# Short filler matmuls left out of the first round of a routing search

## The chip, the cores and the metric

The kernel runs on one core of one Trainium2 chip. The metric is the time of one execution on the device in microseconds (us), and the kernel before has a median of 460.77 us over three runs (459.94, 460.78 and 460.77). One of these executions was also profiled. Where the text names an engine, PE is the matmul engine (TensorE), PEld its weight loads, DVE is VectorE, ACT is ScalarE, POOL is GpSimd and SP is SyncE, which issues most of the DMAs.

## The reference

Two blocks follow each other. The first is a gated linear attention: for each of 4 batches and 8 heads a 48x48 state is decayed and updated over 768 tokens.

```python
f = 1.0 / (1.0 + np.exp(-f_logit))
for t in range(S):
    state = f[:, :, t, :, None] * state + np.einsum('bhd,bhe->bhde', k[:, :, t], v[:, :, t])
    y[:, :, t] = np.einsum('bhd,bhde->bhe', q[:, :, t], state)
```

Its output, as x with 3072 rows of 384, goes into a layer of 8 experts. Each token gets one expert, and each expert takes exactly 384 tokens: all 3072 x 8 logits are walked from the largest to the smallest, and a pair is taken if its token is still free and its expert still has room.

```python
logits = x @ w_gate
for idx in np.argsort(-logits.flatten()):
    tok, e = int(idx) // E, int(idx) % E
    if assigned[tok] >= 0 or counts[e] >= cap:
        continue
    assigned[tok] = e
    counts[e] += 1
for e in range(E):
    out[assigned == e] = np.maximum(x[assigned == e] @ w1[e], 0.0) @ w2[e]
```

## The kernel before

**Attention.** The sequence is cut into 24 chunks of 128 tokens, and a software pipeline of six stages works on them (`attention`). The order of the instructions on PE, DVE, ACT and POOL is written out by hand, so each engine executes in program order and waits only for the semaphores of its operands. A finished chunk's x is copied to DRAM, transposed, and multiplied with the gate weights into `logits` (L387). While the pipeline runs dry, the kernel already prepares the first round of the routing for the 20 tiles of tokens that are done: each token's best logit, its choice of expert and its place on a scale of thresholds (`begin`, `part`, `at_steps`). The last chunk's four tiles follow when its logits arrive, and the 20 others are counted by PE in the meantime (L703); `need` is what is left of the wanted count behind these.

**Routing.** The walk over sorted logits is replaced by seven rounds (`rnd` 0 to 6). In each round every free token proposes to its best open expert, and a search finds the level of logit above which one expert becomes full. The search goes through five digits of the level (`search`). For one digit, `digit_alone` (L770) makes on DVE the comparison `above` with 16 thresholds, lets PE count the choices above each threshold (L780: 24 matmuls of 8 columns, four in the first digit of round 0, because `counted` holds the rest), compares the counts with the wanted number on DVE (`fills`, `filled`), and turns the result into a digit with one matmul of one column (L793). DVE's next comparison reads this digit. `assign` (L857) then marks the tokens above the level, sums them with a matmul (L869) and updates `taken` and `places`. `expert_list` makes the list of the full expert's tokens, starts the load of its weights (L959, SP) and gathers its rows of x (`xe`, L1030, POOL).

**Experts.** `ffn` makes a list of PE pieces for the expert: three transposes of gathered rows (`turn`, L1060), 24 matmuls up (`up`, L1071) and 24 down (`down`, L1083), all of 384 columns in fp32. They go into the queue `pe_work`, and `some(pe_work, n)` takes n pieces of it between the steps of the next rounds' searches. In round 0 there is no expert yet, so `pe_work` is empty until the first list is made.

**Filler.** `idle_turns(n, bank, size)` (L124) issues n matmuls of bf16 ones, `size` columns wide, into a PSUM bank that nobody reads; L127 is their line. Width 384 is used in the attention's start, behind the pieces of the first list (one after each, and 13 behind them) and in two digits of round 1. Width 128 is used in round 0 only: in `digit_alone` 12 ahead of the first digit's counts and 6 ahead of each other digit's counts (L776), 4 ahead of each digit's last matmul (L791), and in `assign` 12 ahead of the sum (L866). That is 12 + 4 x 6 + 5 x 4 + 12 = 68. The condition in `digit_alone` is `not turns[1]`; the first two digits of round 1 have `turns` of (0, 1) and keep their two wide filler matmuls. An exact version of the routing, which uses the same functions, lies behind a condition and does not run on these inputs.

Of the kernel before, what the change touches and what calls it, by code (L numbers as in the profile page):

```python
# [26 lines left out]
def kernel(  # L27
# [32 lines left out]
    nc = tc.nc  # L60
# [12 lines left out]
    CAP = N // E  # L73
# [17 lines left out]
    def const(shape, dtype, name):  # L91
        return consts.tile(shape, dtype, name=name, tag=name)
# [8 lines left out]
    ones = const([128, 128], BF16, "ones")  # L101
    idle = const([128, CAP], BF16, "idle")
# [18 lines left out]
    k_bufs = [kept([128, H, DP], FP32, f"kg{i}") for i in range(NB)]  # L121
    a_bufs = [kept([128, 2, HP, 128], FP32, f"am{i}") for i in range(NB)]

    def idle_turns(n, nothing, size=CAP):  # L124

        for _ in range(n):
            nc.tensor.matmul(out=nothing[:, 0:size], lhsT=ones[:], rhs=idle[:, 0:size], start=True,  # L127
                             stop=True)

    def constants():  # L130
# [67 lines left out]
    def sums(G):  # L198
        g = g_bufs[G["i"] % NB]
        if G["i"] == STAGES - 1:  # L200

            idle_turns(3, ps("nothing", "sum"))
        G["L"] = L = ps("L")
        Lv = L[:, 0:D].rearrange("t (h d) -> t h d", d=DH)
        if "terms" in G:
            for n, term in enumerate(G["terms"]):
                nc.tensor.matmul(out=L[:, 0:D], lhsT=wcum_r[:],
                                 rhs=term[:].rearrange("t h d -> t (h d)"),
                                 start=(n == 0), stop=(n == 1))
        else:  # L210
            nc.tensor.matmul(out=Lv, lhsT=wcum[:], rhs=g[:, :, 0:DH], start=True, stop=True)
# [44 lines left out]
    def columns(G, nm, t):  # L256
        if G["i"] in (1, 2):
            idle_turns(4, ps("nothing", "sum"))
        G[nm + "s"] = T = ps("T")
        for hp in range(HP):  # L260
            nc.tensor.transpose(
                out=T[:, 128 * hp:128 * hp + 128],
                in_=G[t][:, 2 * hp:2 * hp + 2, :].rearrange("t h d -> t (h d)"),
                identity=ident[:])
        G[nm] = work.tile([128, HP, 128], FP32, name=nm, tag=nm, bufs=3)
# [183 lines left out]
    in_order.__enter__()  # L449
    constants()  # L450
    idle_turns(19, ps("nothing", "sum"))
    clamp(chunks[0])
    attention(0, 2)
# [82 lines left out]
    def col(t, *shape):  # L536

        return t.rearrange("p (c o) -> p c o", o=1).to_broadcast((128, NT) + shape)
# [5 lines left out]
    def by_e(t):  # L544

        return t[:].rearrange("p c e -> p e c")

    def rt(shape, name, dtype=FP32, bufs=2):
        return route.tile([128] + shape, dtype, name=name, tag=name, bufs=bufs)
# [4 lines left out]
    def tt(out_, a, b, op):  # L554
        nc.vector.tensor_tensor(out=out_, in0=a, in1=b, op=op)
# [5 lines left out]
    def stt(out_, a, s, b, op0, op1):  # L561
        nc.vector.scalar_tensor_tensor(out=out_, in0=a, scalar=s, in1=b, op0=op0, op1=op1)  # L562

    def reduce(out_, in_, op):
        nc.vector.tensor_reduce(out=out_, in_=in_, axis=AX_X, op=op)
# [143 lines left out]
    def assign_and_run(begun=None, also=None, again=None, exact=None):  # L709
# [5 lines left out]
        def bank(name, tag):  # L715
            return psum.tile([128, 512], FP32, name=name, tag=tag, bufs=BUFS[tag])
# [5 lines left out]
        pe_work, dve_work = deque(), deque()  # L722

        def some(queue, n):
            for _ in range(min(n, len(queue))):
                queue.popleft()()
# [28 lines left out]
        def take(over, pick, level=0.0, op=ALU.is_ge):  # L755
            new = rt([NT], "new")
            stt(new[:], over, level, pick[:], op, ALU.mult)
            tt(taken[:], taken[:], new[:], ALU.add)
# [11 lines left out]
        def digit_alone(above, parts, choice, unit, counted=None, turns=(0, 0)):  # L770

            some(pe_work, turns[0])
            r = bank("cnt", "r")
            cols = [c for c in range(NT) if not counted or c % NCH == NCH - 1]
            if not turns[1]:
                idle_turns(12 if counted else 6, bank("nothing", "O"), 128)  # L776
            for c in cols:
                if c % 8 == 0 and not counted:
                    parts(c, c + 8)
                nc.tensor.matmul(out=r[0:NTH, 0:E], lhsT=above[:, c, :], rhs=choice[:, c, :],  # L780
                                 start=(c == cols[0]), stop=(c == cols[-1]))
            fills = rt([E], "fills")
            tt(fills[0:NTH, :], r[0:NTH, 0:E], counted[1][0:NTH, :] if counted else
               wanted[0:NTH, :], ALU.is_ge)
            filled = rt([1], "filled", BF16)
            reduce(filled[0:NTH, :], fills[0:NTH, :], ALU.max)
            if turns[1]:
                some(pe_work, turns[1])
                idle_turns(2, bank("nothing", "O"))
            else:  # L790
                idle_turns(4, bank("nothing", "O"), 128)  # L791
            digit = r[:, 128:129]
            nc.tensor.matmul(out=digit, lhsT=unit[0:NTH, :], rhs=filled[0:NTH, :], start=True,  # L793
                             stop=True)
            return digit, ALU.add
# [34 lines left out]
        def search(choice, over, digits, slots, first=0, counted=None, alone=()):  # L830


            def less(over, digit, op):
                if digit is None:
                    return over
                new = rt([NT], "over")
                ts(new[:], over[:], digit, op)
                return new

            digit = op = None  # L840
            for n, (steps, unit, size) in enumerate(digits):
                above = counted[0] if counted else rt([NT, NTH], "above", BF16)
                parts = partial(reached, above, over, digit, op, steps)
                if slots and n >= len(alone):
                    parts(0, NT)
                    new = less(over, digit, op)
                    digit, op = digit_beside(above, choice, size, (slots[0] + first, slots[1]))
                    over = new
                else:
                    new, op_new = digit_alone(above, parts, choice, unit, counted,  # L850
                                              *alone[n:n + 1])
                    over = less(over, digit, op)
                    digit, op = new, op_new
                first, counted = 0, None
            return less(over, digit, op) if exact else (over, digit)

        def assign(choice, over, pick, slots):  # L857

            over, level = over
            sure = rt([NT, E], "sure", BF16)  # L860
            stt(sure[:], col(over[:], E), level, choice[:], ALU.is_ge, ALU.mult)
            count = rt([E], "count", BF16)
            with nc.allow_low_precision("counts of at most 24"):
                reduce(count[:], by_e(sure), ALU.add)
            if not pe_work:
                idle_turns(12, bank("nothing", "O"), 128)  # L866
            some(pe_work, slots[0])
            r = bank("sums", "r")
            nc.tensor.matmul(out=r[:, 0:E], lhsT=ones[:], rhs=count[:], start=True, stop=True)  # L869
            some(pe_work, slots[1])  # L870
            take(over[:], pick, level)
            tt(places[:], places[:], r[:, 0:E], ALU.subtract)
# [175 lines left out]
        tiles, turns = iter(range(NT)), iter(range(E))  # L1048
# [52 lines left out]
        with tc.manual_schedule(engines=engines):  # L1101
# [5 lines left out]
            for rnd in range(E - 1):  # L1107
# [15 lines left out]
                else:  # L1123
                    counted = None
                    if rnd == 0:
                        choice, over, pick, _, *counted = begun
                    else:
                        best, pick, masked = picks()
                        choice, over = choices(best, pick, masked)
                        for piece in settle:  # L1130
                            piece()

                    over = search(choice, over, digits, slots, more, counted,
                                  ((0, 1), (1, 1)) if rnd == 1 else ())
                (assign_exact if exact else assign)(choice, over, pick, (3, 5 if rnd == 1 else 7))
                *pieces, used = expert_list(rnd == 0)
                dve_work.extend(pieces)
# [151 lines left out]
    with tc.If(again[0] > 0):  # L1289
# [9 lines left out]
        with tc.For_i(0, B, 1) as b:  # L1299
            x = pool.tile([128, NCH, D], FP32, name="xb", tag="xb", bufs=1)  # L1300
            with tc.For_i(0, HP, 1) as hp:
                scan_pair(pool, x, b, hp)
            nc.sync.dma_start(
                out=xd[0:N, :].rearrange("(b c t) d -> b t c d", b=B, c=NCH)[
                    bass.ds(b, 1)].rearrange("b t c d -> (b t) c d"),
# [13 lines left out]
        out=outs[NT - 1][:, :],  # L1319
# [31 lines left out]
```

## Time and profile before

| what | value |
|---|---|
| median of three runs | 460.77 us (459.94, 460.78, 460.77) |
| time of the profiled execution | 459.94 us |
| its span, first to last instruction | 458.1 us (1.84 us lie around it) |
| PE busy | 443.3 us, 97% of the span |
| DVE busy | 265.7 us, 58% |
| ACT, POOL busy | 139.3 us and 136.1 us, 30% each |
| mean granted TensorE clock | 0.975 of full speed |

The execution has three stretches. Attention lasts to about 151 us. The first round's search and its list of tokens follow. From about 178 us PE works on the experts' matmuls, with the later rounds' searches between them, until 451 us. In the profile a row of the timeline names the start and the duration of a merged group of instructions, its engine, its line, what it writes and reads, how many there are, and in brackets how long the engine had been idle and what ended that. A row of the windows names a stretch, its length, the busy time of each engine with the number of instructions, and the granted clock of PE (1.00 is full speed).

### The profile page before, as it was taken

The numbers are of one execution on the slowest core, as the hardware profiler recorded it, in microseconds if no ns is written. First come the engines' busy times: TensorE is split into PE (matmuls) and PEld (weight loads), VectorE is DVE, ScalarE is ACT, GpSimd is POOL, SyncE is SP. The second block draws the span as 40 slices with busy tenths as digits, with TensorE's granted clock in tenths as the row PEclk, the third lists the DMA queues.
The fourth block names the chain that finished last, engine by engine and source line by source line (L and its number), as shares of the span: only waits on it lengthen the run. The fifth ranks groups of instructions, "written<-read, shape, count | busy, mean of one in ns | idle before, by whom it ended". The sixth has DMA issues, their size and how long they took to land. (4 is left out here: it accounts for less than half of the span.)

```text
span 458.1 us, 12040 instructions
## 1 busy us (share of the span) xinstructions
PE 443.3 (97%) x4961; PEld 299.3 (65%) x4961; DVE 265.7 (58%) x879; ACT 139.3 (30%) x323; POOL 136.1 (30%) x189
## 2 busy tenths in 40 slices
PE   8999999999999989999999999999999999999994
PEld 4788888888887745565565565565565565556552
DVE  5789877788986586657547547647637636000000
ACT  4666666666551001202202212212212212212210
POOL 1566565565550021032032033023023025101001
PEclk9999999999999659999999999999999999999999
DMA  9999989899311036082072072082082087400001
GB/s 160 189 208 208 195 179 207 182 204 193 76 37 54 20 112 217 3 309 69 12 289 80 9 287 84 2 291 86 1 293 74 13 292 240 177 17 34 1 19 39
DMA packets 118400, 59.13 MB, mean 129 GB/s; under 512 B 101664, under 2 KB 112960, under 8 KB 118336
## 3 DMA queue, kind: packets, MB, share of 16 engines
q1 hardware_dynamic: 111760, 44.06, 38.5%
q0 software_dynamic: 3072, 9.44, 6.2%
q10 hardware_dynamic: 3504, 4.77, 3.0%
q8 instruction: 41, 0.67, 0.6%
q14 instruction: 23, 0.19, 0.1%
HBM read 48.77 MB, written 9.49 MB: 127 GB/s over the span
## 5 line engine op out<-in xcount | busy, mean ns | idle before, releaser
L1071 PE MATMUL H<-xeT,w 128*128 128x384 f32 x384 | 132.6, 496 | 0.1
L1071 PEld LDWEIGHTS H<-xeT,w 128*128 128x128 f32 x384 | 69.1, 190 | 45.7 <-issue 4.0
L1083 PE MATMUL O<-w,hT 128*128 128x384 f32 x192 | 67.0, 491 | 0.0
L1083 PE MATMUL last_O<-w,hT 128*128 128x384 f32 x192 | 66.7, 491 | 0.0
L1075 ACT ACTIVATE hT<-H 128x384 f32<-128x384 f32 x64 | 31.4, 491 | 101.3 <-PE H L1071 85.3
L1083 PEld LDWEIGHTS last_O<-w,hT 128*128 128x128 f32 x192 | 35.1, 190 | 23.1 <-issue 2.2
L1083 PEld LDWEIGHTS O<-w,hT 128*128 128x128 f32 x192 | 34.9, 190 | 21.5 <-issue 1.3
L1088 POOL DMA_INDIRECT out_dram<-o,token x21 | 21.3, 1013 | 82.2 <-ACT o L1087 81.3
L324 DVE COPY_PREDICATED am<-mask,A 128x512 f32<-128x512 int32 x48 | 32.3, 725 | 16.2 <-PE A L319 16.2
L988 POOL TENSOR_TENSOR block<-past 128x72 f32<-128x72 f32 x8 | 2.4, 302 | 114.3 <-DVE at L562 101.0
L190 POOL TENSOR_TENSOR low<-g,upper 128x384 fp32r<-128x384 f32 x22 | 22.3, 1014 | 42.5 <-DVE upper L188 38.9
L127 PE MATMUL nothing<-idle,ones 128*128 128x384 bf16 (+1 forms) x142 | 28.4, 354 | 2.4 <-DVE ones L132 1.5
L1063 ACT COPY xeT<-Xe 128x384 f32<-128x384 f32 x24 | 11.4, 480 | 59.7 <-PE Xe L1060 59.4
L334 PE MATMUL Y<-v,am 128*64 128x48 f32 x768 | 27.6, 223 | 1.0 <-DVE am L324 0.9
L334 PEld LDWEIGHTS Y<-v,am 128*64 128x64 f32 x768 | 24.8, 138 | 2.0 <-DVE am L324 1.6
L319 PE MATMUL A<-qT,kT 48*64 48x128 f32 x768 | 25.8, 272 | 0.0
L1030 POOL DMA_INDIRECT xe<-xd,token x21 | 21.5, 1023 | 12.4 <-DVE full L559 5.8
L243 POOL TENSOR_TENSOR kg<-k,ek 128x384 f32<-128x384 f32 x23 | 23.3, 1014 | 2.2 <-ACT ek L221 2.1
L319 PEld LDWEIGHTS A<-qT,kT 48*64 48x64 f32 x768 | 21.0, 133 | 0.4 <-issue 0.3
L127 PEld LDWEIGHTS <-ones 128*128 128x128 bf16 x142 | 14.3, 124 | 9.8 <-issue 6.3
L220 ACT ACTIVATE eq<-dl 128x384 f32<-128x384 f32 x24 | 12.5, 523 | 26.2 <-DVE dl L218 26.1
L1087 ACT COPY o<-O 128x384 f32<-128x384 f32 x12 | 5.7, 479 | 40.7 <-PE O L1083 30.0
(228 smaller groups left out, 668.2 us busy)
## 6 DMA issues: line engine op xcount, KB each, us to landing
w<-in_moe_w_dram SPq DMA_DIRECT2D x16, 1536.0 KB, 6.5
f<-in_f_logit_dram SPq DMA_DIRECT2D x24, 192.0 KB, 5.1
q<-in_q_dram SPq DMA_DIRECT2D x24, 192.0 KB, 5.0
k<-in_k_dram SPq DMA_DIRECT2D x24, 192.0 KB, 4.4
v<-in_v_dram SPq DMA_DIRECT2D x24, 192.0 KB, 5.0
xd<-x ACTq DMA_DIRECT2D x24, 192.0 KB, 2.4
xe<-xd,token POOLq DMA_INDIRECT x21
out_dram<-o,token POOLq DMA_INDIRECT x21
```

The source lines that it names most:

```text
L127: nc.tensor.matmul(out=nothing[:, 0:size], lhsT=ones[:], rhs=idle[:, 0:size], start=True, stop=True)
L190: nc.gpsimd.tensor_tensor(out=low[:], in0=g[:, :, 0:DH], in1=upper[:].bitcast(FP32), op=ALU.subtract)
L220: nc.scalar.activation(out=G["eq"][:], in_=dl[:], func=AF.Exp, bias=0.0, scale=-1.0)
L243: engine.tensor_tensor(out=G["kg"][:, :, 0:DH], in0=G["k"][:], in1=G["ek"][:], op=ALU.mult)
L319: nc.tensor.matmul(out=A[par][HC * j:HC * j + HC, 128 * hp:128 * hp + 128], lhsT=G["kT"][rows, hp, HC * j:HC * j + HC], rhs=G["qT"][rows, ...
L324: nc.vector.copy_predicated(am[:, par], mask[:].unsqueeze(1).to_broadcast((128, HP, 128)), A[par][:].rearrange("s (a t) -> s a t", t=128))
L334: nc.tensor.matmul(out=Y[par][HC * j:HC * j + HC, DH * hp:DH * hp + DH], lhsT=G["am"][:, par, hp, HC * j:HC * j + HC], rhs=G["v"][:, 2 * h ...
L1030: nc.gpsimd.indirect_dma_start(out=xe[:], out_offset=None, in_=xd[:, :], in_offset=bass.IndirectOffsetOnAxis(ap=token[:, i:i + 1], axis=0))
L1071: nc.tensor.matmul(out=L["H"][:, 0:CAP], lhsT=L["w1"][:, d, 128 * ft:128 * ft + 128], rhs=xT[:, d, :], start=(d == 0), stop=(d == DC - 1))
L1075: nc.scalar.activation(out=hT[:, ft, :], in_=L["H"][:, 0:CAP], func=AF.Relu)
L1083: nc.tensor.matmul(out=L["O"][:, 0:D], lhsT=hT[:, ft, 128 * i:128 * i + 128], rhs=L["w2"][:, ft, :], start=(ft == 0), stop=(ft == FC - 1))
L1088: nc.gpsimd.indirect_dma_start(out=outs[next(tiles)][:, :], out_offset=bass.IndirectOffsetOnAxis(ap=L["token"][:, i:i + 1], axis=0), in_=o ...
```

## The change

All 68 filler matmuls of 128 columns are left out, and `idle_turns` loses its argument for the width. The filler of 384 columns stays everywhere. Nothing else is edited; no operation is moved or added.

```diff
-    def idle_turns(n, nothing, size=CAP):
+    def idle_turns(n, nothing):
 
         for _ in range(n):
-            nc.tensor.matmul(out=nothing[:, 0:size], lhsT=ones[:], rhs=idle[:, 0:size], start=True,
+            nc.tensor.matmul(out=nothing[:, 0:CAP], lhsT=ones[:], rhs=idle[:], start=True,
                              stop=True)
...
             cols = [c for c in range(NT) if not counted or c % NCH == NCH - 1]
-            if not turns[1]:
-                idle_turns(12 if counted else 6, bank("nothing", "O"), 128)
             for c in cols:
...
             if turns[1]:
                 some(pe_work, turns[1])
                 idle_turns(2, bank("nothing", "O"))
-            else:
-                idle_turns(4, bank("nothing", "O"), 128)
             digit = r[:, 128:129]
...
                 reduce(count[:], by_e(sure), ALU.add)
-            if not pe_work:
-                idle_turns(12, bank("nothing", "O"), 128)
             some(pe_work, slots[0])
```

## The prediction

> **What bounds the kernel now.** I read the page first, for the clock and the filler's group.
>
> ```profile
> PEclk9999999999999659999999999999999999999999
> ...
> L127 PE MATMUL nothing<-idle,ones 128*128 128x384 bf16 (+1 forms) x142 | 28.4, 354 | 2.4 <-DVE ones L132 1.5
> ```
>
> PE has its full clock everywhere but in two slices, 149 to 172 us: just where the first round's search runs. The 142 filler matmuls include the 68 narrow ones. Next, one row of the windows, from the first expert matmul almost to the end:
>
> ```profile
> 178.46:448.00 269.54, 268.89 (x1117) 156.16 (x1118) 125.45 (x491) 52.42 (x108) 53.50 (x58) 1.00 0.33 116
> ```
>
> PE is busy 268.89 of 269.54 us. So from 178.46 us on PE alone sets the time, and whatever makes this stretch start earlier ends the kernel earlier by as much. Its start hangs on a chain: search, list, gather, first transposes. The transposes wait at 175.10 us for the gathered rows; PE sat idle 0.74 us before them, released by the DMA of xe. The gather and the weights' load are issued from results of the list, the list from the search. So the search of round 0 is on the path, and the timeline must say what ends last in it.
>
> ```profile
> 152.16 0.14 DVE L555 TENSOR_TENSOR need<-wanted,counted 16x8 f32<-16x8 f32 x1
> ...
> 152.36 1.44 PE L127 MATMUL nothing<-idle,ones 128*128 128x128 bf16 x12 [0.66 <-DVE need L555]
> 152.44 0.19 DVE L565 TENSOR_REDUCE pick<-masked 128x4 f32<-128x32 bf16 x1
> ...
> 153.73 0.25 PE L780 MATMUL cnt<-choice,above 128*16 128x8 bf16 x4
> ...
> 154.08 0.15 DVE L555 TENSOR_TENSOR fills<-cnt,need 16x8 f32<-16x8 f32 x1 [1.45 <-PE cnt L780]
> ```
>
> Here the filler itself ends last. The comparison `above` was done at 152.25 us, but the four counts stand behind 12 filler matmuls that start at 152.36 us and take 1.44 us. DVE, finished with `pick` at 152.63, waits 1.45 us. One later digit:
>
> ```profile
> 156.66 0.81 PE L127 MATMUL nothing<-idle,ones 128*128 128x128 bf16 x6
> 156.76 0.89 DVE L562 SCALAR_TENSOR_TENSOR above<-over,cnt,steps 128x128 bf16<-128x128 f32 x3 [0.16 <-PE cnt L793]
> 157.41 0.75 PE L780 MATMUL cnt<-choice,above 128*16 128x8 bf16 x24
> 158.09 0.61 PE L127 MATMUL nothing<-idle,ones 128*128 128x128 bf16 x4
> 158.19 0.15 DVE L555 TENSOR_TENSOR fills<-cnt,wanted 16x8 f32<-16x8 f32 x1 [0.55 <-PE cnt L780]
> 158.38 0.15 DVE L565 TENSOR_REDUCE filled<-fills 16x1 bf16<-16x8 f32 x1
> 158.63 0.18 PE L793 MATMUL cnt<-filled,unit 16*128 16x1 bf16 x1
> 158.85 0.89 DVE L562 SCALAR_TENSOR_TENSOR above<-over,cnt,steps 128x128 bf16<-128x128 f32 x3 [0.16 <-PE cnt L793]
> ```
>
> A digit's period is 158.85 - 156.76 = 2.09 us: `above` 0.89, from its end (157.65) to `fills` 0.54, to the end of `filled` (158.53) 0.34, and 0.32 to the next comparison. Round 1 has a digit with no filler ahead of its counts:
>
> ```profile
> 176.12 0.89 DVE L562 SCALAR_TENSOR_TENSOR above<-over,cnt,steps 128x128 bf16<-128x128 f32 x3 [1.38 <-PE cnt L793]
> 176.53 0.88 PE L780 MATMUL cnt<-choice,above 128*16 128x8 bf16 x24
> ...
> 177.45 0.15 DVE L555 TENSOR_TENSOR fills<-cnt,wanted 16x8 f32<-16x8 f32 x1 [0.44 <-PE cnt L780]
> ```
>
> There the counts start 0.11 us after the first third of `above`, and `fills` comes 0.44 us behind its end. Last, the windows, cut where the clock changes:
>
> ```profile
> 148.71:152.12 3.41, 2.62 (x79) 2.24 (x79) 1.88 (x9) 0.58 (x2) 0.00 (x0) 1.00 0.18 62
> 152.12:155.53 3.41, 3.17 (x36) 2.53 (x35) 1.64 (x9) 0.00 (x0) 0.16 (x3) 0.50 0.00 0
> 155.53:158.95 3.42, 3.42 (x65) 2.75 (x62) 1.94 (x11) 0.00 (x0) 0.00 (x0) 0.50 0.02 5
> ...
> 165.77:169.19 3.42, 2.66 (x30) 1.06 (x29) 3.02 (x8) 0.00 (x0) 1.29 (x2) 0.50 0.29 59
> 169.19:172.60 3.41, 3.35 (x16) 1.43 (x14) 2.97 (x13) 0.00 (x0) 2.13 (x2) 0.50 0.99 405
> ```
>
> The clock falls to 0.50 at 152.12 us, before the first narrow filler matmul runs, and stays there for 20.48 us, though PE counts as busy throughout 155.53 to 158.95. It rises at 172.60, after a stretch filled with matmuls of 384 columns. So the narrow filler runs at half clock, 1.44 us for twelve, and does not bring the clock back.
>
> **The change, part by part.**
>
> *12 matmuls ahead of the first counts.* Without them the counts can start when `above` (152.25) and `need` (152.30) are done, so about 152.36, where the filler starts now. They take 0.25, and `fills` follows 0.10 later (153.98 to 154.08 now): 152.71. DVE is free at 152.63 and not later. Gain 154.08 - 152.71 = 1.37 us. Bounds: 1.2, if the counts wait another 0.2 for their weights, as some rows show ("0.20 <-issue"); 1.4, if `pick` alone decides.
>
> *6 ahead of the counts and 4 ahead of the digit, in four digits.* The six end their weight loads just ahead of the counts' start, so counts for the first third of `above`, ready at 157.06, start at 157.41. By the round 1 rows `fills` would come 0.44 behind `above` in place of 0.54; these ran at full clock, but 24 counts' weight loads take 0.65 to 0.66 us at both clocks, so I take 0.46. Ahead of the digit's matmul the four cost little: from the end of `filled` to the next comparison 0.32 us, in the first digit 0.25 (154.42 to 154.67). I take 0.25. The period becomes 0.89 + 0.46 + 0.34 + 0.25 = 1.94, a gain of 0.15, and four periods (154.67 to 163.02) give 0.60 us. Bounds: 0.2, if only half of the counts' term comes and nothing of the other; 0.7, with 0.44. The four in the first digit end as `filled` ends: no gain.
>
> *12 ahead of the sum.* They run from 162.93 while DVE makes `sure` and `count`. `count` ends at 163.97, the sum starts at 164.17 and `places` at 164.45. Without filler the sum would start some 0.06 behind (191.33 to 191.39 in the next round) and end by 164.21, but `taken` keeps DVE until 164.34. Gain 0.05, bounds 0 and 0.1.
>
> *What follows.* Between `places` and the gather everything hangs on DVE, POOL and SP; the wide filler between it is unedited, and DVE does not wait for it. The weights' load (SP, 166.99) and the gathers (POOL, 170.01) come earlier by the same amount and collide with nothing else: DMA moves 0 to 5 GB/s from 152 to 159 us. Nothing is queued behind a new wait, since none is added. The list and the first transposes keep their length, so the next wait is again the gather's.
>
> Sum: 1.37 + 0.60 + 0.05 = 2.02 us, bounds 1.4 and 2.2, if the clock rises as now. Against the profiled execution, 459.94 us (458.1 of span and 1.84 around it), that is 457.9. This execution was the fastest of the three and lies 0.83 under the median; the other two may carry something that its trace doesn't show. Against the median it is 458.75, which I take.
>
> *The clock.* The three changes in the trace fit a grid: the wide filler's weight loads go from one in 0.32 us to six in 0.94 us at about 5.3 us, and 152.12 and 172.60 lie 43 and 49 steps of 3.413 us behind it. 169.19 to 172.60 is filled with wide matmuls from end to end. In 152.12 to 155.53 the narrow filler streams about 22 times 0.107 us (the twelve's spacing), 2.35 us or 69%, and the clock stayed at half. The share that suffices lies between.
>
> The Trainium skill's page "TensorE: Matmul & The Clock Gate" (Part 1 and "HAM oscillation") speaks against the edit: PE should have no idle gaps above about 3.4 us, or it falls to half clock, and single matmuls of N columns then take (219 + N)/1.2 instead of (398 + N)/2.4 ns. The rows show the fall in spite of the filler, so here the rule has nothing left to protect in the search. If the filler did hold the clock, the rule would charge 20 ns for each of two matmuls in five digits, an estimate of 0.2 us, and the sum would be 1.8. The page also says that the window is free-running, not tied to the program's start; no run here shows that yet.
>
> **The rivals.**
>
> *The rise is missed, and the kernel is slower.* The 14 wide filler matmuls behind the list need 14 x 0.32 = 4.48 us at half clock and start now at 169.18. They would start at 167.16 and end at 171.64. With the grid at the same place, 165.77 to 169.19 would hold 2.03 us of them and two single ones (0.64), 78%, and 169.19 to 172.60 would hold 2.45 us, 72%. Both lie between 69% (not enough) and 100% (enough); where they aren't, PE enters round 1 at half clock. Nine transposes (three in 0.55 us, about 0.13 more each) and four wide filler matmuls (0.16 more each) cost up to 1.8, say 1.5 us. The first expert matmuls, at about 178.0 then, run at half speed to the end of the first filled window, 182.84: (182.84 - 178.0)/2 = 2.4. Together 3.9 against 2.0: slower by 1.9, 461.8 from the profiled execution and 462.7 from the median. For it: the arithmetic of the shares. Against it: it needs the grid at the same place in every run, and three runs of before lie within 0.84 us, so none shows such a loss against another. It decides where the share that suffices is above 78%.
>
> *Half of that.* The clock is caught one window earlier, at 179.43, by the transposes and the first expert matmuls (176.01 to 179.43 has PE busy 3.28 us): 1.5 + 0.7 = 2.2 us, no change, 460.8 to 461.
>
> *Hidden anyway.* The expert stretch could hang on something that doesn't move, as a DMA with its own clock. Both transfers are issued from the list, so I see none: 460.8.
>
> **How the numbers follow.** About 0.2%, 0.92 us, is what can be told from no change. The forecast needs only the serial order on PE and gets 0.62, with its own range of 457.7 (459.94 less 2.2) to 459.4 (median less 1.4). The middle cases together get 0.13, the missed rise 0.25. The range goes down to 457.7 and up into the missed rise, to 462.2, between its two prices.
>
> **What would show it.** Right: `fills` of the first digit within 0.1 us of `pick`'s end, where it is 1.45 us behind now; digit periods of 1.9 to 1.95 us; first transposes about 23.0 us behind the first `need`'s row (152.16) become 20.9; PE from the first expert matmul on as dense and as long as before. Wrong in the steps: digit periods still at 2.09 (then the counts wait for DVE alone), or a first count that waits for something other than `need`. Wrong in the outcome: PEclk at 0.50 beyond the gathered rows' arrival, seen as transposes of far more than 0.55 us for three and expert matmuls at double their 0.34 us spacing.

## The result, and the profile after

The changed kernel has a median of 458.85 us over four runs (457.93 to 459.30), beside 460.77 us before (459.94 to 460.79). The ratio is 0.996 with a 95% interval of 0.9941 to 0.9979. The whole interval lies under 1, so the kernel is faster, by some 0.4%. A later comparison, with 12 runs of after and 23 of before, gave 459.70 and 463.36 us, a ratio of 0.9929 (0.9899 to 0.9959). So the sign is sure, and the size depends on something that the first profile alone does not show. The profile tells it by stages, cut at `need`, at `places`, at the first expert matmul and at the span's end:

| profiled execution | attention, to `need` | search, `need` to `places` | list, to the first expert matmul | experts, to the end | span |
|---|---|---|---|---|---|
| before | 152.16 | 12.29 | 14.01 | 279.6 | 458.1 |
| after | 154.47 | 10.06 | 13.34 | 279.6 | 457.5 |

The search is 2.23 us shorter, the list 0.67. The attention, which the change does not touch, happens to be 2.31 us longer in this execution of after, so the two profiled spans lie only 0.6 us apart. From here on stages are compared, not spans.

The first digit in the timeline after (start and duration in us, engine, line, what is written and read, what ended the idle time before):

```profile
154.47 0.14 DVE L555 TENSOR_TENSOR need<-wanted,counted 16x8 f32<-16x8 f32 x1
...
154.66 0.24 PE L778 MATMUL cnt<-choice,above 128*16 128x8 bf16 x4 [0.66 <-DVE need L555]
154.75 0.19 DVE L565 TENSOR_REDUCE pick<-masked 128x4 f32<-128x32 bf16 x1
...
155.01 0.15 DVE L555 TENSOR_TENSOR fills<-cnt,need 16x8 f32<-16x8 f32 x1
```

The counts now wait for `need` themselves, and `fills` comes 0.54 us behind `need` where it took 1.92. Its row shows no wait any more: PE is done by the time DVE has finished `pick`. A later digit:

```profile
157.53 0.89 DVE L562 SCALAR_TENSOR_TENSOR above<-over,cnt,steps 128x128 bf16<-128x128 f32 x3
157.94 0.88 PE L778 MATMUL cnt<-choice,above 128*16 128x8 bf16 x24 [0.45 <-DVE above L562]
...
158.86 0.15 DVE L555 TENSOR_TENSOR fills<-cnt,wanted 16x8 f32<-16x8 f32 x1 [0.44 <-PE cnt L778]
...
159.45 0.89 DVE L562 SCALAR_TENSOR_TENSOR above<-over,cnt,steps 128x128 bf16<-128x128 f32 x3
```

The period is 159.45 - 157.53 = 1.92 us in place of 2.09. The counts start 0.11 us behind the first third of `above`, as in round 1 before, and PE, busy with filler there before, now waits 0.45 us for DVE. DVE's own wait for the counts shrinks from 0.55 to 0.44 us. The end of the search, before (first fence) and after (second):

```profile
163.02 0.42 DVE L562 SCALAR_TENSOR_TENSOR sure<-over,cnt,choice 128x192 bf16<-128x192 f32 x1 [0.17 <-PE cnt L793]
...
164.16 0.18 DVE L555 TENSOR_TENSOR taken<-taken,new 128x24 f32<-128x24 f32 x1
164.45 0.16 DVE L555 TENSOR_TENSOR places<-places,sums 128x8 f32<-128x8 f32 x1
```

```profile
163.29 0.42 DVE L562 SCALAR_TENSOR_TENSOR sure<-over,cnt,choice 128x192 bf16<-128x192 f32 x1
...
164.29 0.17 PE L863 MATMUL sums<-count,ones 128*128 128x8 bf16 x1 [1.04 <-DVE count L565]
...
164.43 0.18 DVE L555 TENSOR_TENSOR taken<-taken,new 128x24 f32<-128x24 f32 x1
164.53 0.15 DVE L555 TENSOR_TENSOR places<-places,sums 128x8 f32<-128x8 f32 x1
```

From `sure` to `places` it takes 1.24 us in place of 1.43. The clock, in windows around its rise (length; busy time of PE, its loads, DVE, ACT, POOL; clock; DMA share and rate):

```profile
168.70:172.11 3.41, 3.35 (x22) 1.49 (x20) 2.70 (x11) 0.00 (x0) 1.72 (x2) 0.50 0.94 369
172.11:175.52 3.41, 2.81 (x38) 1.73 (x37) 2.14 (x13) 0.30 (x1) 1.45 (x3) 1.00 0.77 259
```

It rises 7.58 us behind `places` (172.11 - 164.53); before it was 8.15 (172.60 - 164.45). The missed rise did not happen here. What did change behind `places` is the gather. The first transposes, before and after:

```profile
175.10 0.55 PE L1060 MATMUL Xe<-ident,xe 128*128 128x128 f32 x3 [0.74 <-DMA xe<-xd,token]
```

```profile
174.55 0.52 PE L1054 MATMUL Xe<-ident,xe 128*128 128x128 f32 x3
```

After, they start 10.02 us behind `places` and wait for no DMA; before they started 10.65 behind and had waited 0.74 us for the rows of xe, though the gathers were issued 5.56 us behind `places` in both. The DMA queues from 172 to 174.6 us, before (first fence) and after (second; queue, kind: packets, MB, share of 16 engines):

```profile
q0 software_dynamic: 136, 0.44, 57.5%
q1 hardware_dynamic: 70, 0.22, 21.0%
q8 instruction: 1, 0.02, 2.3%
```

```profile
q0 software_dynamic: 132, 0.41, 49.4%
q1 hardware_dynamic: 85, 0.28, 26.7%
```

q0 is the gather, q1 the weights. The shares of both differ somewhat, but only one queue is there before and missing after: a packet of instructions, 16384 bytes, travels beside the gather before. The experiments below follow this up.

### The profile page after: what moved, and what is told of

The parts are those of the page before. It is cut to its first block, busy times and chain, and to the rows that moved or that the text cites. A ratio compares the mean times of both kernels' runs of the same rounds, so it can differ in the third digit from the quotient of the medians.

```text
span 457.5 us, 11904 instructions
## 1 busy us (share of the span) xinstructions
PE 436.2 (95%) x4893; PEld 293.6 (64%) x4893; DVE 265.8 (58%) x879; ACT 139.6 (31%) x323; POOL 136.5 (30%) x189
## 5 line engine op out<-in xcount | busy, mean ns | idle before, releaser
L127 PE MATMUL nothing<-idle,ones 128*128 128x384 bf16 x74 | 18.7, 388 | 1.6 <-DVE ones L132 1.5
L237 DVE TENSOR_TENSOR qg<-q,eq 128x384 f32<-128x384 f32 x24 | 17.5, 730 | 0.6 <-ACT eq L220 0.6
```

Of the source, the lines that this page charges most:

```text
L127: nc.tensor.matmul(out=nothing[:, 0:CAP], lhsT=ones[:], rhs=idle[:], start=True, stop=True)
L237: nc.vector.tensor_tensor(out=G["qg"][:, :, 0:DH], in0=G["q"][:], in1=G["eq"][:], op=ALU.mult)
```

## Experiments: each part alone

Each of the first four kernels is the kernel before with one part of the narrow filler taken out. Each was run once, in 463.94, 461.64, 461.04 and 460.91 us beside 464.89 for the kernel before. These times follow the attention first (`need` at 157.30, 155.27, 155.22 and 154.86 us), so the stages are read and not the times.

**The 12 ahead of the first counts.**

```diff
-            if not turns[1]:
+            if not turns[1] and not counted:
                 idle_turns(12 if counted else 6, bank("nothing", "O"), 128)
```

> The kernel before without the 12 narrow filler matmuls ahead of the first digit's counts; all other filler stays. Stage measured: from the start of DVE's need to the start of places, 12.29 us before and 10.06 us after the whole change. Theory (filler stands serially ahead of work that others wait for): fills 0.5 to 0.6 us behind need in place of 1.92, the stage 10.9 us, digit periods still 2.09 us. Rival (the time lies in the clock or in the spread between executions, not in the queue): the stage stays near 12.3 us, or it shortens by other rows than this one.

```profile
157.30 0.14 DVE L555 TENSOR_TENSOR need<-wanted,counted 16x8 f32<-16x8 f32 x1
...
157.85 0.15 DVE L555 TENSOR_TENSOR fills<-cnt,need 16x8 f32<-16x8 f32 x1
```

0.55 us from `need` to `fills`; the search takes 10.94 us, 1.35 less than before, and later digits keep their 2.09. So these 1.35 us are the filler's place in PE's queue.

**The 6 ahead of the later counts.**

```diff
-            if not turns[1]:
+            if not turns[1] and counted:
                 idle_turns(12 if counted else 6, bank("nothing", "O"), 128)
```

> The kernel before without the 6 narrow filler matmuls ahead of the counts in digits two to five. Theory: counts start as the first third of above is done, fills 0.45 us behind the end of above in place of 0.54, digit period 2.00 us, the stage from need to places 12.29 less 0.36 = 11.9 us. Rival (the counts wait for DVE alone, the four ahead of the digit cost the 0.15): period still 2.09 us, stage 12.3 us.

```profile
159.77 0.89 DVE L562 SCALAR_TENSOR_TENSOR above<-over,cnt,steps 128x128 bf16<-128x128 f32 x3 [0.16 <-PE cnt L793]
161.10 0.15 DVE L555 TENSOR_TENSOR fills<-cnt,wanted 16x8 f32<-16x8 f32 x1 [0.44 <-PE cnt L780]
...
161.76 0.89 DVE L562 SCALAR_TENSOR_TENSOR above<-over,cnt,steps 128x128 bf16<-128x128 f32 x3 [0.17 <-PE cnt L793]
```

The period is 1.99 us and the search 11.88, 0.41 less than before, as expected.

**The 4 ahead of each digit.**

```diff
-            else:
-                idle_turns(4, bank("nothing", "O"), 128)
```

> The kernel before without the 4 narrow filler matmuls ahead of each digit's last matmul. Theory: from the end of filled to the next comparison 0.26 us in place of 0.32, digit period 2.03 us, the stage 12.29 less 0.25 = 12.05 us; the first digit gains nothing. Rival (the six ahead of the counts cost it all, since they run later and end as before): period 2.09 us, stage 12.3 us.

```profile
156.53 0.15 DVE L555 TENSOR_TENSOR fills<-cnt,need 16x8 f32<-16x8 f32 x1 [0.85 <-PE cnt L780]
...
161.07 0.89 DVE L562 SCALAR_TENSOR_TENSOR above<-over,cnt,steps 128x128 bf16<-128x128 f32 x3
162.51 0.15 DVE L555 TENSOR_TENSOR fills<-cnt,wanted 16x8 f32<-16x8 f32 x1 [0.55 <-PE cnt L780]
...
163.10 0.89 DVE L562 SCALAR_TENSOR_TENSOR above<-over,cnt,steps 128x128 bf16<-128x128 f32 x3
```

The period is 2.03 us, as expected: `fills` is as late as before, the digit 0.06 us earlier. The search as a whole took 11.33 us and not 12.05, because in this execution the clock fell only behind the first 12, at 157.23 us: `fills` came 1.31 us behind `need` (155.22), not 1.92, and the second digit's counts still ran with 0.44. So the 12 cost 1.38 us at half clock and 0.77 (1.31 less 0.54) at full clock.

**The 12 ahead of the sum.**

```diff
-            if not pe_work:
-                idle_turns(12, bank("nothing", "O"), 128)
```

> The kernel before without the 12 narrow filler matmuls ahead of the sum over the chosen tokens. The prediction had 0.05 us for it; the trace after has 1.24 us from the start of sure to the start of places in place of 1.43. Theory (these 12 alone held the sum): 1.24 us, the stage from need to places 12.1 us. Rival (the 0.19 us came from other filler that is gone, or from the clock): still 1.38 to 1.43 us, stage 12.25 us or more.

```profile
165.00 0.42 DVE L562 SCALAR_TENSOR_TENSOR sure<-over,cnt,choice 128x192 bf16<-128x192 f32 x1 [0.16 <-PE cnt L793]
...
166.24 0.15 DVE L555 TENSOR_TENSOR places<-places,sums 128x8 f32<-128x8 f32 x1
```

1.24 us: these 12 alone held the sum by 0.19. (The search took 11.38 us, since here too the clock fell behind the first 12.)

**Twice the dose ahead of the first counts.** The kernel before with 24 in place of 12.

> The kernel before with 24 narrow filler matmuls in place of 12 ahead of the first digit's counts, a dose of twice the size. Theory (serial queue on PE): fills moves later by 12 times the spacing of a filler matmul, 12 x 0.107 = 1.28 us where PE has half its clock, 12 x 0.055 = 0.66 us where it has full clock; from need to fills 3.2 us at half clock, 2.0 at full, something between if the clock falls on the way. Rival (the filler hides under DVE's work or under the wait for the pool's banks): 1.92 us or less, unchanged.

```profile
156.67 2.72 PE L127 MATMUL nothing<-idle,ones 128*128 128x128 bf16 x24 [0.66 <-DVE need L555]
```

`fills` comes at 159.68, 3.20 us behind `need` (156.48): each further filler matmul costs its 0.107 us in full. The one run took 467.87 us. The windows of this kernel add something:

```profile
156.59:160.01 3.42, 3.34 (x32) 2.94 (x31) 0.62 (x5) 0.00 (x0) 0.16 (x3) 0.50 0.00 0
177.07:180.48 3.41, 1.99 (x32) 1.15 (x30) 2.44 (x14) 0.00 (x0) 1.76 (x3) 1.00 0.81 272
```

The first window holds 24 + 4 narrow matmuls, 28 x 0.107 = 3.0 us or 88% of it, and behind it the clock did rise, at 160.0. It fell again at 163.4. The second window, behind the later rise at 177.1, has PE busy for only 1.99 of 3.41 us, and at its end the clock fell once more, just ahead of the transposes: they took 0.90 us for three in place of 0.55. So here dense narrow filler brought the clock back, where 69% as in before did not, and a rise that was followed by a hole was lost. Where between 69% and 88% the border lies was not measured.

## Experiments: the clock's rise, and the rest of the filler

**The price of a missed rise.** The kernel after without the 13 wide filler matmuls behind the list.

```diff
                 if rnd == 0:
-                    idle_turns(13, bank("nothing", "O"))
```

> The kernel after without the 13 wide filler matmuls behind the list of round 0 (the seven single ones stay). This prices the rival of the prediction, the missed rise of the clock. By that rival's sum: the clock stays at 0.50 through the transposes and into the expert matmuls, from places to the first expert matmul 14.8 us in place of 13.3, from there to the span's end 282.0 in place of 279.6, together 3.9 us (bounds 2.2 and 4.5). If the wide filler is not what brings the clock back: the clock rises within 3.4 us as after, and both stretches stay within 0.3 us.

```profile
176.40 0.87 PE L1054 MATMUL Xe<-ident,xe 128*128 128x128 f32 x3
...
181.05 2.94 PE L1065 MATMUL H<-xeT,w 128*128 128x384 f32 x6
```

The transposes ran at half clock and the list took 14.66 us (181.05 less `places` at 166.39), 1.3 more than after, close to the 1.5 of the rival. The experts took 280.4 us, only 0.7 more than after: the clock rose at 182.6, 1.5 us behind the first expert matmul, in a window that they did not fill alone. So the missed rise cost 2.1 us in this execution (463.21 us in all, with `need` at 156.32), not 3.9.

**The pairs in round 1.** The kernel after without the two wide filler matmuls ahead of the first two digits of round 1.

```diff
                 some(pe_work, turns[1])
-                idle_turns(2, bank("nothing", "O"))
```

> The kernel after without the two pairs of wide filler matmuls ahead of the digits' matmuls in round 1. Theory (any filler ahead of a matmul that DVE waits for costs its own length): those matmuls start 0.3 to 0.45 us earlier each, the first expert matmul 12.6 to 12.9 us behind places in place of 13.3, and the time falls by 0.4 to 0.7 us against the kernel after. Rival (these pairs keep the clock up, or the gathered rows land too late to use the gain): the transposes wait for the DMA of xe and the gain is under 0.2 us, or the clock falls to 0.50 before the expert matmuls and the kernel is 1 to 4 us slower than after.

```profile
178.65 2.20 PE L1064 MATMUL H<-xeT,w 128*128 128x384 f32 x6 [0.46 <-ACT xeT L1056]
```

The first expert matmul came 13.02 us behind `places`, 0.32 earlier than after and less than expected: the second and third transposes both start 0.32 us earlier, so the first pair cost its length, but ahead of the expert matmul PE now waited 0.46 us for ACT's copy of the last rows, and the second pair's share was lost there. The time is 460.32 us over 12 runs (ratio to before 0.9936, 0.9908 to 0.9963) against 459.70 for the kernel after beside it: no gain can be seen, and 2 of the 12 had a mean clock of at most 0.972, which none of 12 of after had. The theory held for the first pair in the queue, and not for the time.

**The kernel after again**, in the same comparison.

> The kernel after, unchanged, in five rounds beside the kernel before. Theory: ratio to before 0.995 to 0.997, the stage from need to places 10.06 us again, less if the clock happens to fall later. Rival (the first comparison was luck of the attention's length): ratio within 0.998 to 1.002.

The ratio was 0.9929 (0.9899 to 0.9959), a larger gain than expected: 3.66 us between the medians. The stages were as after: search 10.07 us, list 13.34. The runs of before differed among each other: 9 of 23 had a mean clock of at most 0.972, and these took 464.8 us in the mean, the other 14 took 462.3. So the kernel before was profiled twice more.

> The kernel before, unchanged, profiled once more, to see where its clock stands in another execution. In the comparison of five rounds the kernel after gained 3.7 us at the medians where the queue on PE accounts for 2.2, and 9 of 23 executions of before had a mean clock of at most 0.972 while none of 12 of after had less than 0.974. Theory (the narrow filler also disturbs the clock): in an execution with a mean clock of at most 0.972 the clock rises early, in the search or at the start of the wide filler, falls again before the gathered rows are there, and the transposes (0.9 us for three in place of 0.55) and the first expert matmuls run at half clock, some 2 to 4 us; in one with 0.974 or more the clock has one rise, and the stage from need to places takes 11.4 to 12.3 us. Rival (only the attention differs between executions): the clock has a single rise in any case, and what is left of the difference lies ahead of need.

> The kernel before, unchanged, profiled a further time; the same as for the first look. Of two looks one or two should show a mean clock of at most 0.972 if 9 in 23 holds (chance 0.6).

Both had a mean clock of 0.972, in 463.64 and 464.16 us. The windows of the first, cut where its clock changes, and its third group of transposes:

```profile
172.80:176.21 3.41, 3.41 (x12) 1.47 (x10) 3.17 (x15) 0.00 (x0) 2.80 (x3) 0.50 0.97 370
176.21:179.62 3.41, 2.92 (x53) 2.06 (x52) 1.49 (x7) 0.96 (x2) 0.12 (x2) 1.00 0.86 234
179.62:183.03 3.41, 3.41 (x19) 2.08 (x18) 1.89 (x8) 0.48 (x1) 0.00 (x0) 0.50 0.88 327
```

```profile
179.87 0.90 PE L1060 MATMUL Xe<-ident,xe 128*128 128x128 f32 x3
```

The clock rises at 176.21, is lost one window later, and the end of the list and the first expert matmuls run at half clock. In the window between, PE had waited 0.49 us for the gathered rows. Against after (10.07, 13.34 and 279.6 us for search, list and experts), this execution has 11.92, 14.46 and 280.4 us: 1.85 + 1.12 + 0.7 = 3.7 us. The second look has 11.70, 14.45 and 280.7: 1.63 + 1.11 + 1.1 = 3.8 us. In the first profile of before it was 2.23 + 0.67 = 2.9 us. So behind `need` before loses 2.9 to 3.8 us, beside the 3.66 between the medians. The rival's single rise of the clock falls, but the attention differs too, and by more: these two executions are 3.7 and 4.2 us longer than the first profile's 459.94, and 2.9 and 3.2 us of that lie ahead of `need` (155.07 and 155.40 against 152.16). The search even cost less here than in the first profile, because the clock fell later (1.53 and 1.31 us from `need` to `fills`). What they lose more than the first profile in the stages lies behind `places`.

## Experiments: the block of instructions

In the trace, the instruction queue q8 moves 16384 bytes at a time, 41 times before and 40 after, and from one such block to the next some 126 matmuls start with their loads. They are PE's program, as the table shows: matmuls that are taken out ahead of it move the next block. Where a block starts, in us behind `places`, and how long the first transposes waited for xe:

| kernel | matmuls out | block behind `places` | wait for xe |
|---|---|---|---|
| 24 in place of 12 | -12 | 7.65 | 1.00 |
| before, three profiles | 0 | 8.24, 8.17, 8.34 | 0.74, 0.49, 0.55 |
| without the first 12 | 12 | 11.2 | 0; the third group 1.12 |
| without the 12 of the sum | 12 | 11.2 | 0; the third group 0.12 |
| without the 4s | 20 | 14.0 | 0 |
| without the 6s | 24 | 14.0 | 0 |
| after, two profiles | 68 | 15.4, 15.2 | 0 |

The two kernels made from after, without the 13 and without the pairs, have it at 15.5 and 15.1 and wait for nothing either.

The Trainium skill's page "Runtime: NRT & Kernel Launch" ("Instruction fetch mechanics") has these blocks, 16 KiB or 256 instructions that an engine's sequencer fetches by itself over its own DMA queue, and calls the cost mostly hidden. Size and spacing agree with this trace. That the fetch is hidden from PE says nothing on the other transfers that it meets.

The last two kernels move the block without touching the search. The 34 wide filler matmuls at the attention's start and ahead of its last sums are each split into three of 128 columns, the same columns in 68 matmuls more.

```diff
-    idle_turns(19, ps("nothing", "sum"))
+    split_turns(19, ps("nothing", "sum"))
...
+    def split_turns(n, nothing):
+        for _ in range(3 * n):
+            nc.tensor.matmul(out=nothing[:, 0:128], lhsT=ones[:], rhs=idle[:, 0:128], start=True,
+                             stop=True)
```

**The kernel after with the block put back.**

> The kernel after, with the 34 wide filler matmuls at the attention's start and before its last sums each split into three of 128 columns: the same streamed columns, but 68 matmuls (136 instructions) more ahead of the search, as many as the change took out. PE's instructions arrive by DMA in blocks of 16384 bytes, about 126 matmuls with their weight loads; in three looks at the kernel before one block starts 8.2 to 8.3 us behind places, beside the gather, and the first transposes wait 0.5 to 0.7 us for xe; after, no block starts between -1.8 and 15 us and they wait for nothing. Theory (the narrow filler's second cost is where it puts this block): with the split a block starts 8 to 8.5 us behind places again, the transposes wait 0.5 to 0.7 us, the stage from need to places stays at 10.06 us, in some executions the clock has a hole there (mean clock of at most 0.972), and the median lies 1 to 2 us above the kernel after's 459.7 us. Rival (the gather is late by the filler's heat or by chance): no such wait, the median within 0.5 us of the kernel after's.

```profile
179.15 0.55 PE L1060 MATMUL Xe<-ident,xe 128*128 128x128 f32 x3 [0.86 <-DMA xe<-xd,token]
```

The block starts 8.31 us behind `places` (168.35) and the transposes wait 0.86 us. The search takes 10.08 us as after, the list 14.15 in place of 13.34. So the position of the block is enough to make the gather late, with no narrow filler in the search. The mean clock was at most 0.972 in 2 of 12 runs.

**The kernel before with the block moved away.**

> The kernel before with the same split: all its narrow filler in the search stays, but 136 instructions more lie ahead, so the block of instructions starts some 68 matmuls sooner, in the search, and the next about 58 later, behind the gather. Theory: no block between about -2 and 14 us behind places, no wait for xe, the stage from need to places 11.4 to 12.3 us as before, mean clocks of 0.974 and more in nearly all executions, and the median 1 to 2 us under the kernel before's (ratio 0.996 to 0.998). Rival (it is the filler in the search that disturbs the gather or the clock): as the kernel before, ratio 0.999 to 1.001.

```profile
178.49 0.55 PE L1066 MATMUL Xe<-ident,xe 128*128 128x128 f32 x3
```

No block starts between 1.8 us ahead of `places` (168.28) and 15.3 behind it. There is no wait for xe, though all the narrow filler is in the search, so the filler alone does not make the gather late. The list takes 13.56 us, and the mean clock is at most 0.972 in 1 of 12 runs, where it was so in 12 of 22 runs of before beside it.

The times of both kernels missed what was expected. With 463.55 us (ratio to before 1.0014, 0.9988 to 1.0040) and 463.75 us (1.0016, 0.9991 to 1.0042) neither differs from before. For the first that fits in sign, but it lies 3.9 us above the kernel after's 459.70 (measured in another comparison), more than the 1 to 2 expected. For the second the gain is missing altogether. The edit seems not to be neutral ahead of the search: `need` comes at 158.27 and 156.57 us, where eleven of the other twelve profiles have it at 152.2 to 156.5. The matmuls at the start are not the reason: 57 narrow ones take 5.71 us with the clock's first rise at 6.46 us, and 19 wide ones take 5.66 with the rise at 6.38 (the profile without the first 12), or 4.91 where it comes at 4.86 (after). What is, stays open. So the stages decide on the gather, and the worth of the block in the whole time was not measured by itself.

## Why the prediction was right, and where not

The predicted 458.75 us stands against 458.85, inside the range of 457.7 to 462.2, and the forecast case, faster, came true.

- *The 12 ahead of the first counts*, 1.37 us: 1.38 between the two profiles, 1.35 alone. Right where the clock falls ahead of them; 0.77 in executions where it falls behind them, a case outside the stated bounds of 1.2 to 1.4.
- *The 6 and the 4 in four digits*, 0.60 us: 0.66 (7.69 us from the first `above` of the later digits to `sure`, in place of 8.35). The period is 1.92 where 1.94 was taken. The 6 alone gave 0.41, the 4 alone 0.06 a digit.
- *The 12 ahead of the sum*, 0.05 us, bounds 0 and 0.1: measured 0.19. The step that failed is that `taken` keeps DVE until its end: after, `places` starts 0.08 us ahead of the end of `taken` (164.43 + 0.18), and 0.14 us of the 0.19 come from there. Whether the sum or `taken` then let it start, its row, which shows no wait, does not tell.
- *What follows*: "The list and the first transposes keep their length" and the gathers "collide with nothing else" were wrong. The list became 0.67 us shorter, and the first transposes came 20.08 us behind `need` (174.55 - 154.47), where 20.9 was forecast. I had asked what data moves beside the gather, and not where PE's own instructions arrive.
- *The missed rise*: neither profile of after has it, and two of three of before lose their rise again, the other way round than the rival had it. Its price was mis-sized by the term of the first expert matmuls, 2.4 us, which measured 0.7; the term of the list, 1.5, measured 1.3. Its grid was not at the same place in each execution either: the wide filler's loads at the start speed up at 5.29 us before and at 4.65 us after, which agrees with the Trainium skill's page "TensorE: Matmul & The Clock Gate" (Part 1), that the window is free-running.
- *The base*: behind `need` the two first profiles differ by 2.23 + 0.67 = 2.90 us, 0.9 more than the sum of 2.02; the two median differences, 1.92 and 3.66 us, lie on both sides of it. That the prediction hit to 0.1 us is therefore in part luck: the attention, unedited, ended between 152.2 and 157.3 us in the profiles that leave it alone, a spread larger than the change. What makes it so was not settled.

Open: why a low mean clock is more frequent in before (21 of 45 runs in the two larger comparisons) than in the split kernels, which have either the block beside the gather (2 of 12) or the narrow filler (1 of 12). After without the pairs, which has neither, shows it in 2 of 12 too. Both together may be needed; neither that nor how the narrow filler would add to it was shown.

## What to carry to other kernels

Filler on an in-order engine is work: read whether what stands behind it is waited for, and charge its full length, at the clock that the engine has there. Before keeping filler for the clock's sake, look whether the clock's rows change at all in its stretch; thin filler (69% of a window here) cost its time and bought nothing, while the dense wide filler ahead of the experts was worth 2.1 us in the one execution without it. Instructions also have to be fetched: adding or removing some dozens of them moves where the next block of code arrives, and a latency-bound transfer many microseconds later can be hit by it, as the gather was here some 8 us behind `places`.

## What the runs showed of the hardware

- A 16384-byte block of PE's instructions beside an indirect gather kept the first transposes of its rows waiting for 0.5 to 1.0 us (0.86 where the block was put there by moving it). In two profiles with a block 11.2 us behind `places`, the third group of rows was waited for, 1.12 and 0.12 us.
- The clock fell to 0.50 behind windows in which PE was busy for 2.92 and for 2.62 of 3.41 us (the second ahead of the search before, with no pause of PE as long as 1 us), and stayed at 1.00 behind one with 2.81: busy time by itself does not tell what the gate counts. It rose behind a window with some 88% of streaming narrow filler (one execution) and not behind one with 69%.
- The counts of 8 columns kept their pace at half clock: `fills` follows `above` by 0.44 to 0.45 us at both.
